# Block products of the output projection by seven in place of eight, with both weights' parts streamed

## The chip, the cores and the metric

The kernel runs on one core of one Trainium2 chip. The core has a matrix engine (PE; PEld is its loading of weights), three engines for element-wise work (DVE, ACT, POOL) and a queue, SP, from which every DMA of this kernel is issued. The metric is the device time of one execution in microseconds (us).

## The reference

```python
a = softmax(phi, over 32 slots)                    # (8 batches, 8 heads, 576 tokens, 32)
k_m, v_m = a^T k, a^T v                            # 32 slots x 64 per head
attn = softmax(q k_m^T / 8) v_m                    # (8, 8, 576, 64)
x = attn, heads side by side                       # (4608, 512)
h = x @ w_in                                       # (4608, 2048)
g = where(h > 0, h, exp(min(h, 0)) - 1)            # elu
return g @ w_out                                   # (4608, 512)
```

The weights arrive as float64; all else is float32.

## The kernel before

**Three passes.** Each large product is made of two-part numbers. A value is split into a high part (a cast to fp32r) and a low part (the value less its high part), and the product is summed over three passes: low x high, high x low, high x high. Splitting a tensor thus costs one cast on ACT and one subtraction on DVE.

**Units of work.** A batch of 576 tokens is two halves of 288. The 2048 hidden channels are 16 groups `j` of 128. One unit `it` is one (batch, half, group), and a batch is 32 units. For each unit, `hidden(it)` (L657) makes 128 channels x 288 tokens in PSUM with 6 matmuls of 288 columns. `elu_exp` (L672, L673) and `elu_max` (L684 for 256 tokens, L686 for the last 32, the "rest") form g. `elu_high` (L698) and `elu_low` (L704) split it into `gp`. `project(it)` (L712) multiplies the two 128-token blocks of `gp` with the group's 128 x 512 tile of w_out: 2 blocks x 3 passes = 6 matmuls of 512 columns. The 32-token rests of two batches are gathered and projected together after each odd batch (`rest_high`, `rest_low`, `rest_project`, 48 matmuls, then `rest_store`).

**PSUM.** `hidden` has two banks (`psh`). Its bank is free again when `elu_max` has read it. The attention has two (`psb`). The projection has four (`pso00` to `pso11`), one for each half and token block, since the halves of a batch alternate group by group.

**The product w_in with the values.** `vw` (L502) multiplies the 32 slot values of each head with w_in in four chunks `c` of 512 hidden channels (`win`, resident in SBUF); `vw_high` (L605) and `vw_low` (L611) split it. `hidden` multiplies that with the softmax `A`, so the attention's own output is never formed.

**Attention of a batch**, `attention(b, o)`: `load_phi`, `load_kv` (5 loads), `load_e` (3), `spread_max` (the slots' maxima go to DRAM as `nmd`, L276, and come back to all partitions as `nmb`, L278), `e_shift` on POOL (L289), `e_exp` on ACT (L294), `slots` on PE (L453), `scores` on PE (L502), then the softmax on DVE and ACT for three token ranges `u`.

**Order.** The list `FIRST` is a hand-written order for units 0 to 63 (batches 0 and 1, and the decoding of both weights from float64). After it, `plan` sorts every step by a place number, counted in units:

```python
    def attention(b, o):
        at(o - 4, load_phi, b)
        for c in range(NCH):
            at(o - 3 + c, load_kv, b, c)
...
        at(o + 1, spread_max, b)
...
            at(o + 5.4, slots, b, c)
```

For batch `b` with first unit `base = 32 b`, `o` is `base - 22`. PE and SP carry out their steps in exactly this order. ACT, DVE and POOL get an order from the scheduler, which may move a step ahead of an earlier one. SP issues a DMA as soon as its buffer is free and its data is there; the place numbers do not hold it back, and one that must wait holds all behind it.

Of the kernel before, what the change touches and what calls it, by code (L numbers as in the profile page):

```python
# [8 lines left out]
F32 = mybir.dt.float32  # L9
F32R = mybir.dt.float32r  # L10
# [86 lines left out]
elu_high.16 rest_copy.16 collect.14.0 elu_low.16 project.15 elu_exp.17 load_raw.15 dec_add.13
collect.14.1 elu_max.17 dec_high.13 vw.0.1.256.512 dec_top.14 rest_copy.17 collect.15.0 hidden.18
elu_high.17 dec_rest.13 collect.15.1 project.16 elu_exp.18 elu_low.17 vw_high.0.1.256.512
elu_max.18 hidden.19 dec_low.14 rest_copy.18 vw_low.0.1.256.512 elu_high.18 project.17 dec_add.14  # L100
elu_exp.19 load_raw.16 elu_low.18 dec_mag.15 load_raw.17 elu_max.19 load_raw.18 hidden.20
dec_high.14 dec_top.15 rest_copy.19 load_raw.19 elu_high.19 project.18 elu_exp.20 elu_low.19
dec_low.15 elu_max.20 vw.1.1 dec_rest.14 elu_high.20 rest_copy.20 dec_mag.16 elu_low.20 hidden.21
vw_high.1.1 dec_add.15 project.19 dec_top.16 elu_exp.21 dec_high.15 elu_max.21 load_raw.20
hidden.22 dec_mag.17 vw_low.1.1 rest_copy.21 elu_high.21 project.20 dec_low.16 elu_low.21
elu_exp.22 dec_rest.15 dec_mag.18 hidden.23 elu_max.22 dec_add.16 dec_mag.19 rest_copy.22
project.21 elu_high.22 dec_top.17 elu_exp.23 dec_mag.20 hidden.24 load_raw.21 elu_max.23
dec_low.17 elu_low.22 rest_copy.23 hidden.25 dec_top.18 elu_high.23 elu_exp.24 project.22
elu_exp.25 elu_max.24 dec_low.18 elu_max.25 rest_copy.24 hidden.26 elu_low.23 elu_high.24
rest_copy.25 elu_high.25 collect.22.0 dec_mag.21 project.23 collect.22.1 elu_exp.26 elu_low.24  # L110
elu_max.26 hidden.27 collect.23.0 elu_high.26 rest_copy.26 project.24 collect.23.1 elu_exp.27
elu_low.25 elu_low.26 elu_max.27 hidden.28 dec_add.17 elu_high.27 rest_copy.27 project.25
elu_low.27 elu_exp.28 dec_add.18 hidden.29 elu_max.28 dec_top.19 elu_high.28 rest_copy.28
project.26 elu_exp.29 elu_low.28 dec_low.19 elu_max.29 load_raw.22 hidden.30 dec_add.19
elu_high.29 rest_copy.29 project.27 elu_low.29 elu_exp.30 dec_top.20 load_raw.23 vw.1.2 elu_max.30
dec_low.20 dec_top.21 rest_copy.30 project.28 load_raw.25 elu_high.30 vw_high.1.2 dec_add.20
dec_low.21 hidden.31 vw_low.1.2 dec_high.20 project.29 elu_exp.31 elu_low.30 dec_mag.23 elu_max.31
hidden.32 dec_mag.22 dec_rest.20 rest_copy.31 elu_high.31 dec_add.21 project.30 dec_mag.25
elu_exp.32 elu_low.31 dec_top.22 dec_high.21 hidden.33 elu_max.32 project.31 dec_low.22
dec_rest.21 rest_copy.32 elu_high.32 dec_add.22 elu_exp.33 hidden.34 elu_max.33 dec_high.22  # L120
vw.0.2.0.256 elu_low.32 rest_copy.33 elu_high.33 dec_top.23 hidden.35 elu_exp.34 project.32
vw_high.0.2.0.256 elu_max.34 elu_exp.35 elu_low.33 rest_copy.34 elu_high.34 vw_low.0.2.0.256
hidden.36 dec_low.23 elu_max.35 load_raw.30 project.33 elu_low.34 elu_exp.36 rest_copy.35
dec_add.23 load_raw.24 elu_high.35 hidden.37 elu_max.36 dec_high.23 elu_low.35 rest_copy.36
elu_high.36 dec_rest.22 project.34 elu_exp.37 elu_low.36 dec_mag.30 elu_max.37 hidden.38
dec_rest.23 elu_high.37 rest_copy.37 load_raw.27 project.35 elu_low.37 elu_exp.38 dec_mag.24
dec_top.25 hidden.39 elu_max.38 dec_low.25 load_raw.28 dec_top.24 project.36 rest_copy.38
elu_high.38 elu_exp.39 elu_low.38 dec_low.24 hidden.40 elu_max.39 dec_mag.27 dec_add.25
rest_copy.39 project.37 elu_high.39 dec_add.24 elu_exp.40 dec_mag.28 load_raw.26 hidden.41
elu_max.40 load_raw.29 elu_low.39 elu_high.40 rest_copy.40 dec_top.28 project.38 elu_exp.41  # L130
elu_max.41 vw.0.2.256.512 dec_low.28 collect.38.0 rest_copy.41 project.39 elu_high.41 collect.38.1
vw_high.0.2.256.512 dec_mag.26 elu_low.40 vw_low.0.2.256.512 hidden.42 dec_mag.29 collect.39.0
project.40 elu_exp.42 collect.39.1 elu_max.42 elu_low.41 hidden.43 elu_high.42 rest_copy.42
dec_add.28 project.41 elu_exp.43 elu_low.42 dec_high.28 dec_top.30 hidden.44 elu_max.43 dec_low.30
dec_rest.28 project.42 rest_copy.43 elu_high.43 dec_top.27 elu_exp.44 hidden.45 elu_max.44
dec_low.27 vw.0.3.0.256 elu_low.43 rest_copy.44 dec_top.26 elu_high.44 hidden.46 elu_exp.45
project.43 vw_high.0.3.0.256 load_raw.31 elu_max.45 elu_exp.46 vw_low.0.3.0.256 rest_copy.45
elu_high.45 hidden.47 dec_low.26 elu_max.46 elu_low.44 rest_copy.46 elu_high.46 hidden.48
elu_low.45 elu_exp.47 elu_low.46 project.44 elu_exp.48 elu_max.47 dec_add.26 rest_copy.47
elu_max.48 hidden.49 dec_mag.31 dec_add.27 rest_copy.48 elu_high.47 project.45 load_phi.2  # L140
dec_top.29 elu_exp.49 vw.0.3.256.512 elu_max.49 dec_low.29 elu_low.47 project.46 rest_copy.49
dec_add.30 elu_high.48 vw_high.0.3.256.512 vw_low.0.3.256.512 hidden.50 dec_high.30 elu_high.49
elu_low.48 project.47 dec_rest.30 elu_exp.50 elu_low.49 elu_max.50 load_kv.2.0 hidden.51
dec_add.29 rest_copy.50 elu_high.50 dec_top.31 load_kv.2.1 dec_high.29 project.48 elu_exp.51
load_kv.2.2 elu_low.50 dec_low.31 load_kv.2.3 hidden.52 elu_max.51 dec_rest.29 elu_high.51
rest_copy.51 load_kv.2.4 project.49 elu_exp.52 elu_low.51 elu_max.52 vw.1.3 dec_add.31
# [29 lines left out]
def fused_kernel(ctx: ExitStack, tc: tile.TileContext, phiT, phi, kv0, kvt, kv, q0, q1, w_in, w_out, out):  # L176
# [22 lines left out]
    def t2k(shape, name):  # L199
        return work.tile(shape, F32, name=name, tag="t2k", bufs=7)  # L200
# [732 lines left out]
```

## Time and profile before

| | |
|---|---|
| median of 3 runs | 734.49 us (734.39 to 738.01) |
| profiled execution, its own time | 735.4 us |
| its span, first to last instruction | 733.6 us |
| PE busy | 709.2 us, 97% |
| DVE, ACT, POOL busy | 467.2, 465.0, 44.6 us |
| DMA, mean | 88 GB/s |

A line of the profile names the engine, the line of the code, what is written and read (`out<-in`), the shapes and the count. In a timeline the first column is the start, the second the time taken by the merged instructions, and a bracket at the end is idle time of the engine and what ended it. The recorded end of a matmul contains its drain, so the time that a group costs PE is read from its start to the start of the next group.

### The profile page before, as it was taken

How to read it: one execution, taken by the hardware profiler on the slowest of the kernel's cores; microseconds unless marked ns; L12 is line 12 of the kernel's file. 1: busy time of each engine (PE TensorE's matmuls, PEld its weight loads, DVE VectorE, ACT ScalarE, POOL GpSimd, SP SyncE). 2: the span in 40 equal slices, each digit the busy share in tenths (PEclk: the TensorE clock that was granted, in tenths of full speed). 3: DMA queues.
4: the chain of work that ended last, by engine and by line, in shares of the span. 5: the costliest groups of instructions: out<-in, count | busy, mean ns of one | idle time of the engine just before them, and what ended most of it. 6: DMA issues, size and time to landing. Idle time of an engine off the chain costs nothing.

```text
span 733.6 us, 13668 instructions
## 1 busy us (share of the span) xinstructions
PE 709.2 (97%) x5114; PEld 572.5 (78%) x5114; DVE 467.2 (64%) x1253; ACT 465.0 (63%) x1110; POOL 44.6 (6%) x88
## 2 busy tenths in 40 slices
PE   7688999999999999999999999999999999999997
PEld 6566888888768878877788777887787887888885
DVE  4999899886495467544954449545774447754442
ACT  4768988886456656755655557656565565665552
POOL 0001112123000100010000100000000010000000
PEclk9899999999999999999999999999999999999999
DMA  8960513431316110611015210260002600010002
GB/s 311 370 231 28 203 30 115 149 101 62 101 59 210 28 44 1 239 42 45 2 57 182 56 45 1 75 206 28 18 1 75 218 27 20 1 58 0 2 1 72
DMA packets 24978, 64.46 MB, mean 88 GB/s; under 512 B 3408, under 2 KB 7632, under 8 KB 24912
## 3 DMA queue, kind: packets, MB, share of 16 engines
q1 hardware_dynamic: 24912, 63.59, 25.7%
q8 instruction: 41, 0.67, 0.4%
q14 instruction: 25, 0.20, 0.1%
HBM read 54.13 MB, written 9.44 MB: 87 GB/s over the span
## 4 chain that ended last, share of the span: by engine, by line
PE 68%; DMA 14%; DVE 8%; ACT 5%; issue 2%; POOL 1%; SPq 1%; POOLq 0%; DVEq 0%; ACTq 0%
PE pso L712 41%; PE psh L657 21%; DMA nmd<-nm 6%; PE psb L502 4%; DMA nmb<-nmd 3%; PE psb L453 2%; DMA ph<-phiT 2%; POOL e L289 1%; DMA win<-w_in 1%; ACT gf L673 1%; DMA kvt<-kv 1%; ACT gf L672 1%; DMA e<-phi 1%; DVE gf L681 1%; DVE nm L407 1%
## 5 line engine op out<-in xcount | busy, mean ns | idle before, releaser
L712 PE MATMUL pso<-wout,gp 128*128 128x512 f32 x1728 | 449.6, 398 | 3.3 <-DVE gp L704 2.6
L712 PEld LDWEIGHTS pso<-wout,gp 128*128 128x128 f32 x1728 | 310.1, 188 | 84.2 <-ACT gf L673 13.0
L657 PEld LDWEIGHTS psh<-A,vw 128*128 128x128 f32 x1536 | 229.9, 189 | 39.5 <-issue 6.2
L657 PE MATMUL psh<-A,vw 128*128 128x288 f32 x1536 | 251.1, 299 | 8.6 <-DVE rest L686 3.8
L684 DVE SCALAR_TENSOR_TENSOR gf<-gf,psh 128x256 f32<-128x256 f32 x192 | 80.4, 419 | 130.3 <-ACT gf L673 130.0
L672 ACT ACTIVATE gf<-psh 128x288 f32<-128x288 f32 x256 | 104.7, 409 | 86.3 <-PE psh L657 84.4
L698 ACT CAST gp<-gf 128x256 fp32r<-128x256 f32 x256 | 103.4, 404 | 87.0 <-DVE gf L684 73.4
L704 DVE TENSOR_TENSOR gp<-gf,gp 128x256 fp32r<-128x256 f32 x256 | 107.6, 421 | 55.0 <-ACT gp L698 54.7
L673 ACT ACTIVATE gf<-gf 128x288 f32<-128x288 f32 x256 | 113.7, 444 | 7.8
L611 DVE TENSOR_TENSOR vw<-psb,vw 128x512 fp32r<-128x512 f32 (+2 forms) x74 | 43.3, 602 | 11.7 <-ACT vw L605 11.5
L289 POOL TENSOR_TENSOR e<-e,nmb 128x512 f32<-128x512 f32 (+1 forms) x18 | 19.7, 1122 | 377.1 <-DMA nmb<-nmd 374.8
L681 DVE SCALAR_TENSOR_TENSOR gf<-gf,psh 128x288 f32<-128x288 f32 x64 | 28.9, 452 | 18.2 <-ACT gf L673 16.9
L605 ACT CAST vw<-psb 128x512 fp32r<-128x512 f32 (+2 forms) x74 | 37.1, 522 | 2.9 <-PE psb L502 0.7
L502 PE MATMUL psb<-win,kvm 64*32 64x512 f32 (+2 forms) x592 | 36.0, 541 | 0.0
L694 POOL COPY rest<-gf 128x32 f32<-128x32 f32 x64 | 24.3, 380 | 167.6 <-DVE gf L681 167.5
L686 DVE SCALAR_TENSOR_TENSOR rest<-gf,psh 128x32 f32<-128x32 f32 x192 | 34.2, 179 | 0.1
L752 ACT CAST gp<-rest 128x256 fp32r<-128x256 f32 x32 | 13.0, 406 | 23.8 <-PE pso L712 21.8
L373 DVE SCALAR_TENSOR_TENSOR top<-mag,top 128x512 uint32<-128x512 uint32 x32 | 22.2, 692 | 1.9 <-ACT mag L364 0.3
L757 DVE TENSOR_TENSOR gp<-rest,gp 128x256 fp32r<-128x256 f32 x32 | 13.4, 418 | 15.0 <-ACT gp L752 14.9
L368 ACT ACTIVATE mag<-raw 128x512 uint32<-128x512 uint32 x30 | 20.0, 670 | 2.5 <-DVE top L373 2.5
L294 ACT ACTIVATE e<-e 128x512 f32<-128x512 f32 (+1 forms) x18 | 9.8, 559 | 16.9 <-POOL e L289 16.8
L364 ACT ACTIVATE mag<-raw 128x512 f32<-128x512 f32 x30 | 19.5, 668 | 0.4 <-DVE win L385 0.4
(96 smaller groups left out, 368.4 us busy)
## 6 DMA issues: line engine op xcount, KB each, us to landing
kvt<-kv SPq DMA_DIRECT2D x32, 512.0 KB, 7.4
out<-osb SPq DMA_DIRECT2D x16, 512.0 KB, 2.8
raw<-w_in SPq DMA_DIRECT2D x15, 512.0 KB, 6.0
raw<-w_out SPq DMA_DIRECT2D x15, 512.0 KB, 7.9
qt<-q SPq DMA_DIRECT2D x18, 384.0 KB, 4.3
ph<-phiT SPq DMA_DIRECT2D x7, 576.0 KB, 5.0
e<-phi SPq DMA_DIRECT2D x12, 256.0 KB, 6.3
qh<-q SPq DMA_DIRECT2D x4, 576.0 KB, 11.5
```

What stands on the lines that cost most here:

```text
L502: nc.tensor.matmul(outs[a][32 * j : 32 * j + 32, :], lhs[r, 32 * j : 32 * j + 32], rhs[r, j], start=True, stop=True, tile_position=(64 * a ...
L605: nc.scalar.copy(s["vw"][c][:, HI, a, n0:n1], ps)
L611: nc.vector.tensor_tensor(t[:, LO, a, n0:n1], ps, t[:, HI, a, n0:n1], ALU.subtract)
L657: nc.tensor.matmul(ps, t[:, x, g, c0 : c0 + P], s["A"][hf][:, y, g, :], start=(n == 0), stop=(n == 5),)
L672: nc.scalar.activation(gf, ps, AF.Relu, scale=-1.0)
L673: nc.scalar.activation(gf, gf, AF.Exp, scale=-1.0)
L681: nc.vector.scalar_tensor_tensor(gf, gf, -1.0, ps, ALU.add, ALU.max)
L684: nc.vector.scalar_tensor_tensor(gf[:, :n], gf[:, :n], -1.0, ps[:, :n], ALU.add, ALU.max)
L686: nc.vector.scalar_tensor_tensor(rest_of(b, j)[:, o : o + REST], gf[:, n:], -1.0, ps[:, n:], ALU.add, ALU.max)
L698: nc.scalar.copy(gp[:, HI], gs[it][:, : NT * P])
L704: eng.tensor_tensor(gp[:, LO], gf[:, : NT * P], gp[:, HI], ALU.subtract)
L712: nc.tensor.matmul(ps, gp[:, y], wout[j][:, x, :], start=(first and n == 0), stop=(last and n == 2),)
```

## The change

Batches 0 and 1 stay as they are but for where buffers lie. In batches 2 to 7:

- **Halves in turn.** All 16 groups of half 0 come before those of half 1.
- **Pairs of groups.** Two groups (256 channels) are one step. `elu_relu` runs for each, `elu_exp2` once over both (576 columns), `elu_max2` for each. `project2` is at the second unit of the pair.
- **Seven products.** The two token blocks and the two channel groups make a 2 x 2 block matrix; the tile of w_out (256 x 512) is 2 x 2 as well. `project2` forms the output from seven block products of 256 columns in place of eight: 7 x 3 passes = 21 matmuls of 256 columns, against 12 of 512. Pairs 3 and 7 of each half (`PLAIN`) and the first half of batch 2 keep 12 of 512. So 11 halves x 6 pairs = 66 pairs use seven.
- **Sums of g.** `sums` makes four 128-column sums on POOL. `direct_parts` splits three blocks (ACT and DVE, 256 and 128 columns), `sum_parts` the sums (512 columns).
- **Sums of w_out.** While units 42 to 63 and the rests of batches 0 and 1 run, `build_full`, `build_sums` (POOL, 2 of 512 and 4 of 256 columns), `build_high` (ACT, 2 of 512) and `build_low` (DVE, 2 of 512) make the four sums of each of 8 pairs, and `save_t` writes them to DRAM (1 MB each).
- **Streams.** `load_t` brings a pair's sums back before each of the 66 pairs (1 MB each) into two buffers used alternately, so it waits for the last reader of the pair before the previous one. `save_w` writes decoded w_in to DRAM, and `load_w` brings it back for each of batches 2 to 7 in 8 loads of 512 KB; `vw` is then made in two halves of 256 columns. All four `vw` chunks of a batch are now made within 16 units.
- **PSUM.** The four banks hold one half: R, C, D, S. `collect_first` and `collect_sums` take R and S after pair 6, `collect_last` adds C and D after pair 7.

Core of the diff:

```diff
-        for hf, j in turns if len(order) == 0 else [
-            (hf, j) for j in range(j0, j1) for hf in range(2)
-        ]:
+        units_of = [(hf, j) for j in range(j0, j1) for hf in range(2)]
...
+        elif b >= NB:
+            units_of = [(hf, j) for hf in range(2) for j in range(j0, j1)]
...
+    def load_t(it):
+        t = work.tile(
+            [P, 2, 4, Q], F32R, name="tt", tag=f"wb{turn_of('tt', 2)}", bufs=1
+        )
+        nc.sync.dma_start(
+            t.rearrange("p x a n -> p (x a n)").bitcast(U32), td[order[it][2] // 2]
+        )
...
+    def sums(it):
...
+        eng = nc.gpsimd
+        eng.tensor_tensor(S[:, 0], a21, a22, ALU.add)
+        eng.tensor_tensor(S[:, 2], a11, a21, ALU.subtract)
+        eng.tensor_tensor(S[:, 1], S[:, 0], a11, ALU.subtract)
+        eng.tensor_tensor(S[:, 3], a12, S[:, 1], ALU.subtract)
...
+    def project2(it):
...
+        M = {
+            1: ("R", 0, A(0), Bt(0, 0)),
+            2: ("C", 0, A(1), Bt(1, 0)),
+            3: ("C", 1, SS(3), Bt(1, 1)),
+            4: ("D", 0, A(2), TT(4)),
+            5: ("S", 0, SS(0), TT(1)),
+            6: ("R", 1, SS(1), TT(2)),
+            7: ("S", 1, SS(2), TT(3)),
+        }
+        after_rest = p == 0 and hf == 0 and b % 2 == 0
+        for n in (2, 4, 5, 7, 3, 1, 6) if after_rest else (1, 2, 4, 6, 5, 7, 3):
...
         for c in range(NVC):
-            products(b, c, base - 7.6 + 8 * c)
+            for h in range(2):
+                at(base - 13 + 4 * c + h, load_w, b, c, h)
+            products(b, c, base - 10 + 4 * c)
+    streamed = [it for it in range(1, len(order), 2) if order[it][0] >= NB and seven(it)]
+    for n, it in enumerate(streamed):
+        at(streamed[n - 2] + 1.7 if n > 1 else it - 10 + n, load_t, it)
...
+            x = it - 3.5
+            if b % 2 == 0 and hf == 0 and 1 < j < 4:
+                x = it - j - 1 + 0.665 + 0.0001 * j
+            at(x, hidden, it)
+            at(x + 0.00001, elu_relu, it)
+            if j % 2:
+                at(x + 0.00002, elu_exp2, it)
+                at(x + 0.00003, elu_max2, it - 1)
+                at(x + 0.00004, elu_max2, it)
...
+                at(x + 0.1, direct_parts, it)
+                if seven(it):
+                    at(x, sums, it)
+                    at(x + 0.2, sum_parts, it)
+                at(it + 0.6, project2, it)
```

The attention's places are unchanged (`o = base - 22`).

More of the change, by code (lines that the diff above doesn't have):

```diff
@@ L138 @@
[L138 to L143, printed above, removed]
@@ L150 @@
[L150 to L151 removed]
+save_w.0.0 save_w.0.1 scores.1.0 dec_low.7 scores.1.1.yz elu_max.4 elu_exp.2 turn.1.0 rest_copy.4
+hidden.5 elu_high.4 turn.1.1 softmax_max.1.0 vw.0.0.384.512 elu_exp.5 softmax_max.1.1
+scores.1.2.yz elu_max.2 vw_high.0.0.384.512 softmax_shift.1.0 rest_copy.2 elu_high.2
+vw_low.0.0.384.512 softmax_exp.1.0 elu_low.2 hidden.6 elu_max.5 softmax_shift.1.1 rest_copy.5
@@ new lines @@
+load_kv.2.4 project.49 elu_exp.52 elu_low.51 elu_max.52 vw.1.3 dec_add.31 rest_copy.52 elu_high.52
+phi_max.2 dec_high.31 project.50 vw_high.1.3 elu_low.52 spread_max.2 build_high.3 dec_rest.31
+phi_exp.2.0 hidden.53 vw_low.1.3 phi_exp.2.1 project.51 build_low.3 save_t.3 elu_exp.53
+slot_scale.2 build_full.4 build_sums.4 elu_max.53 hidden.54 elu_high.53 rest_copy.53 elu_low.53
+project.52 elu_exp.54 elu_max.54 hidden.55 load_e.2.0 elu_high.54 rest_copy.54 elu_low.54
+project.53 build_high.4 elu_exp.55 load_e.2.1 elu_max.55 load_q.2.1 hidden.56 elu_high.55
@@ new lines @@
+build_full.6 build_sums.6 elu_low.58 slots.2.0 elu_exp.59 project.57 load_q.2.0 elu_max.59
+elu_high.59 rest_copy.59 elu_low.59 slots.2.1 hidden.60 load_q.2.2 slots.2.2 load_w.2.0.0
+elu_exp.60 project.58 elu_max.60 elu_high.60 rest_copy.60 elu_low.60 slots.2.3 load_w.2.0.1
+build_high.6 hidden.61 slots.2.4 load_w.2.1.0 elu_exp.61 project.59 build_low.6 slots_copy.2
+save_t.6 elu_max.61 elu_high.61 rest_copy.61 build_full.7 build_sums.7 hidden.62 elu_low.61
+project.60 elu_exp.62 elu_max.62 hidden.63 elu_high.62 rest_copy.62 elu_low.62 slots_transpose.2
@@ L705, in elu_low, with seven, build_full @@
         gps[it] = gp
+        let_go("gf", it)
+    Q = CW // 2
+    NP = NJ // 2
+    PLAIN = (3, 7)
+    late = {}
+    fulls = {}
+    prods = {}
+    tts = {}
+    def seven(it):
+        b, hf, j = order[it]
+        return (b, hf) != (NB, 0) and j // 2 not in PLAIN
+    def build_full(p):
+        if "FE" not in late:
+            late["FE"] = work.tile([P, 2, 4, Q], F32, name="FE", tag="wb1", bufs=1)
+        F = late["FE"][:, 0]
+        for n in range(2):
+            w = wout[2 * p + n]
+            nc.gpsimd.tensor_tensor(
+                F[:, 2 * n : 2 * n + 2].rearrange("p a n -> p (a n)"), w[:, HI], w[:, LO], ALU.add
+            )
@@ new lines, in elu_relu, with elu_exp2, elu_max2 @@
+    def elu_relu(it):
+        if "G" not in late:
+            late["G"] = [
+                work.tile([P, 2, 2, HALF], F32, name="G", tag="osb0", bufs=2) for _ in range(2)
+            ]
+        n = it // 2 % 4
+        G = late["G"][n // 2][:, n % 2]
+        nc.scalar.activation(G[:, it % 2], gs[it], AF.Relu, scale=-1.0)
+        gs[it] = G, gs[it]
+    def elu_exp2(it):
+        G = gs[it][0].rearrange("p k n -> p (k n)")
+        nc.scalar.activation(G, G, AF.Exp, scale=-1.0)
+    def elu_max2(it):
+        b, hf, j = order[it]
+        G, ps = gs[it]
+        G = G[:, it % 2]
+        n = NT * P
+        nc.vector.scalar_tensor_tensor(G[:, :n], G[:, :n], -1.0, ps[:, :n], ALU.add, ALU.max)
+        o = (b % 2 * 2 + hf) * REST
+        nc.vector.scalar_tensor_tensor(
+            rest_of(b, j)[:, o : o + REST], G[:, n:], -1.0, ps[:, n:], ALU.add, ALU.max
+        )
```

423 lines of the change are left out of this document (298 added, 125 removed).

## The prediction

> **What bounds the kernel now.** I read the page's busy times and chain first, then PE's timeline in the steady part, then stretches of time by engine.
>
> ```profile
> span 733.6 us, 13668 instructions
> PE 709.2 (97%) x5114; PEld 572.5 (78%) x5114; DVE 467.2 (64%) x1253; ACT 465.0 (63%) x1110; POOL 44.6 (6%) x88
> PE 68%; DMA 14%; DVE 8%; ACT 5%; issue 2%; POOL 1%; SPq 1%; POOLq 0%; DVEq 0%; ACTq 0%
> q1 hardware_dynamic: 24912, 63.59, 25.7%
> ```
>
> ```profile
> 399.77 1.55 PE L712 MATMUL pso<-wout,gp 128*128 128x512 f32 x6
> 401.15 0.96 PE L657 MATMUL psh<-A,vw 128*128 128x288 f32 x6
> 401.95 1.55 PE L712 MATMUL pso<-wout,gp 128*128 128x512 f32 x6
> ```
>
> ```profile
> 145.00:160.00 15.00, 15.00 (x109) 12.29 (x108) 13.74 (x32) 12.83 (x32) 3.41 (x8) 1.00 0.34 106
> 444.00:462.00 18.00, 18.00 (x132) 14.48 (x122) 15.87 (x47) 12.41 (x30) 0.00 (x0) 1.00 0.01 1
> 600.00:690.00 90.00, 90.00 (x644) 73.03 (x644) 52.30 (x152) 54.40 (x129) 0.00 (x0) 1.00 0.06 22
> ```
>
> The columns of the last fence are PE, PEld, DVE, ACT, POOL, granted clock, DMA share, GB/s. PE has no gap: between the starts, `hidden` costs it 0.80 us and `project` 1.38. DVE and ACT have room on average (52 and 54 of 90 us), but not everywhere: while a batch's softmax runs (444 to 462), DVE is at 15.87 of 18. DMA moved 63.59 MB in 25.7% of 733.6 us, 337 GB/s while it worked. So fewer PE columns are worth their time, as long as PE still finds its operands.
>
> **1. The products (gain).** `hidden` takes 0.80/6 = 0.133 us for 288 columns, `project` 1.38/6 = 0.230 for 512: 0.43 ns a column and a fixed part of 8 ns. 256 columns come to 0.119. A pair of seven is 21 x 0.119 = 2.50 against 12 x 0.230 = 2.76, so 0.26 us less, on 66 pairs 17 us. In proportion to 512 columns (0.115) it would be 0.345 a pair, 23 us; if a narrow matmul took no less than the 288 columns do (0.133), 21 x 0.133 = 2.79 and the gain is gone. I take 17: both shapes lie on one line and 256 is next to 288. PLAIN pairs and rests are unchanged.
>
> **2. SP and the attention's chain (loss).** Before, nothing holds SP back, so a batch's loads run far ahead. The chain is in the critical path's view (start, us, what), and the first `e_exp` in the timeline:
>
> ```profile
> 227.36 8.24 DMA nmd<-nm
> 235.66 4.50 DMA nmb<-nmd
> 241.59 2.02 POOL e L289 x2
> 243.63 0.42 ACT e L294
> 255.29 2.46 PE psb L453 x80
> ```
>
> ```profile
> 169.32 0.34 SPq L276 DMA_DIRECT2D nmd<-nm  x1
> 172.48 0.33 SPq L278 DMA_DIRECT2D nmb<-nmd  x1
> 241.66 0.63 ACT L294 ACTIVATE e<-e 128x512 f32<-128x512 f32 x1 [1.99 <-POOL e L289]
> ```
>
> From the issue of `nmd` to the first `e` ready (241.66 + 0.63) it takes 14.9 us, and `slots` came 13.0 us after that. With a quiet queue `nmd` took 3.2 us (169.32 to 172.48, when SP issued `nmb`), and the same chain would be 9.9.
>
> After the change `load_t` stands in that queue. Offsets are in units from the next batch's `base`. In order, SP has `load_t` for the pair at -21 (place -25.3), `load_kv` and `load_e`, `load_t` for -19 (place -21.3), the last `load_kv`, then `spread_max` (-21). The load for -19 takes the buffer that the pair at -23 reads, so SP stands until that pair's last product with a sum, and `nmd` goes out about 1.0 us later (two issues). From there PE has only the pair's last three matmuls (0.36), five `hidden` (4.0) and two `project2` (5.0) to `slots` at -16.6: 9.4 us. So `slots` stands 1.0 + 14.9 - 9.4 = 6.5 us if `nmd` takes 8.24, and 1.5 if it takes 3.2. Ahead of `nmd` are 1 MB of sums, a `kv` of 0.25 MB and what is left of some 3.6 MB (1 of sums, 4 x 0.5, 0.6 of `e`) issued in the 8.5 us before, more like the busy case, so I take 5.5. Batch 2's attention is in `FIRST`, and batch 3's falls in the half without sums; batches 4 to 7 remain: 4 x 5.5 = 22 us, between 6 and 26. Behind `nmb` on SP wait later `load_t`s, but those pairs are two or more away.
>
> **3. The clock.** A standing PE also loses clock:
>
> ```profile
> 24.00:27.50 3.50, 3.15 (x54) 2.38 (x54) 3.40 (x7) 3.18 (x7) 0.21 (x1) 0.63 1.03 412
> ```
>
> Amid the early waits 3.5 us were granted 0.63, a loss of 1.3 us. Four long stands: 4 us, between 0 and 5. The Trainium skill (TensorE: Matmul & The Clock Gate, Part 1) says that an idle window of some 3.4 us halves the clock until a busy one has passed; by that rule four stands cost an estimated 7 us, and the sum would be 3 us higher. Half clocks in the early rows agree.
>
> **4. `load_w` behind a store.** `vw` of chunk 3 (place base + 2) needs the second half of its w_in, whose load stands at base + 0, behind `store` (base - 0.2).
>
> ```profile
> 378.98 2.58 SPq L743 DMA_DIRECT2D out<-osb  x2
> out<-osb SPq DMA_DIRECT2D x16, 512.0 KB, 2.8
> kvt<-kv SPq DMA_DIRECT2D x32, 512.0 KB, 7.4
> ```
>
> `store` waits for `collect_last`, about 1.0 us after the half's last matmul, and takes SP 1.3; the load then lands 2.8 later when alone, at about 5.1, or 5.9 behind the store's bytes. PE is at `vw` after two `hidden` and one `project2`, 4.1. So 1.0 to 1.8 us for batches 3 to 7; at 7.4 to land it would be 5.6 a batch. The queue is nearly empty there, so 1.4 x 5 = 7 us, between 0 (if PE is late anyway) and 28. The start of batch 2 is alike: its chunk 2 waits on SP behind `save_t` of the last sums and two stores, 2 us, between 0 and 4.
>
> **5. `vw` in two halves.** 512 columns cost 1.02 us from start to start, 192 (in `scores`) 0.48:
>
> ```profile
> 318.58 1.09 PE L502 MATMUL psb<-win,kvm 64*32 64x512 f32 x16
> 319.60 1.65 PE L712 MATMUL pso<-wout,gp 128*128 128x512 f32 x6
> 438.57 0.56 PE L502 MATMUL psb<-qt,kvm 64*32 64x192 f32 x16
> 439.05 1.07 PE L657 MATMUL psh<-A,vw 128*128 128x288 f32 x6
> ```
>
> Between them 256 is 0.59, twice 1.18: 0.16 more for 24 chunks, 4 us, unless the second half follows without the fixed part. I take 2, between 0 and 4.
>
> **6. The PSUM banks and DVE.** A bank of `hidden` is freed by `elu_max2`, now behind an exponential over 576 columns:
>
> ```profile
> 425.59 0.96 PE L657 MATMUL psh<-A,vw 128*128 128x288 f32 x6
> 426.59 0.41 ACT L672 ACTIVATE gf<-psh 128x288 f32<-128x288 f32 x1 [0.41 <-PE psh L657]
> 427.04 0.44 ACT L673 ACTIVATE gf<-gf 128x288 f32<-128x288 f32 x1
> 427.51 0.42 DVE L684 SCALAR_TENSOR_TENSOR gf<-gf,psh 128x256 f32<-128x256 f32 x1 [0.86 <-ACT gf L673]
> 427.85 0.18 DVE L686 SCALAR_TENSOR_TENSOR rest<-gf,psh 128x32 f32<-128x32 f32 x1
> 245.51 1.04 PE L657 MATMUL psh<-A,vw 128*128 128x288 f32 x6 [0.81 <-DVE rest L686]
> ```
>
> PE is done with `hidden` at 426.39; the bank is free 1.64 us later, at 428.03. With 288 columns more in the exponential (0.20 by the slope between the two casts below) it is 1.85, about 2.0 with the hand-over, and PE comes back for that bank after one `project2`, 2.50. Before it came back after 3.6. The last row shows such a wait already, when ACT stood behind `e`. The margin of 0.5 us is less than one cast or subtraction:
>
> ```profile
> L673 ACT ACTIVATE gf<-gf 128x288 f32<-128x288 f32 x130 | 57.7, 444 | 3.9
> L672 ACT ACTIVATE gf<-psh 128x288 f32<-128x288 f32 x131 | 53.6, 409 | 51.8 <-PE psh L657 50.7
> L698 ACT CAST gp<-gf 128x256 fp32r<-128x256 f32 x131 | 53.1, 405 | 51.7 <-DVE gf L684 49.7 <-PE pso L712 2.0
> L605 ACT CAST vw<-psb 128x512 fp32r<-128x512 f32 x32 | 18.8, 587 | 1.5
> L611 DVE TENSOR_TENSOR vw<-psb,vw 128x512 fp32r<-128x512 f32 x32 | 21.8, 682 | 8.4 <-ACT vw L605 8.3
> L289 POOL TENSOR_TENSOR e<-e,nmb 128x512 f32<-128x512 f32 x6 | 7.7, 1309 | 256.7 <-DMA nmb<-nmd 256.7
> ```
>
> Per pair of seven, ACT has 2 x 0.41 + 0.65 + 0.405 + 0.31 + 0.59 = 2.8 us (0.31 for 128 columns by the slope from 512 to 256), DVE 4 x 0.30 for the maxima + 0.42 + 0.28 + 0.68 = 2.6, in 4.1 us of PE; before they had 2.5 and 2.0 in 4.4. POOL, a quarter of 1.31 and a start, 4 x 0.45 = 1.8. All fit. In the softmax's 18 us DVE would need 15.9 + 4.4 x 0.6 = 18.5, which is over. I take 1 us for each of 5 batches, 5 us, between 0 and 19 (0.2 for each of 96 pairs).
>
> **7. The sums of w_out.** Each of 8 adds 2 x 0.587 to ACT, 2 x 0.68 to DVE and some 5.6 to POOL. POOL has room; in 145 to 160 DVE has 13.74 of 15 and three builds bring 4.1, so 2.8 too much there, some of it taken up later: 2 us, between 0 and 5. `save_w` and `save_t` are nothing while the queue has room (0.34 busy in that stretch).
>
> **8. DMA in total.** 66 MB of sums and 25 of w_in in, 12 out, and the old 64 make some 170 MB (in units of 1.05 MB for 1 MB), at 337 GB/s some 505 us of 760: not the bound. A pair's sums need 1.05/0.337 = 3.1 us and about 1.5 to land where 5.7 are at hand, two such loads a half; nothing, if no other load is ahead, and inside term 2 where one is.
>
> **Sum.** -17 + 22 + 4 + 7 + 2 + 2 + 5 + 2 = +27. The profiled execution took 735.4 (span 733.6 and 1.8 around it), 0.9 above the median, so 762 against it and about 761 as a median. With all ends at their best -23 + 6 = -17, 718; the likeliest's own range, terms 2, 4 and 6 going part of the way, is 743 to 785.
>
> **Rivals.**
> - **The waits find cover: faster.** If `nmd` finds a quiet queue and PE reaches `slots` late enough, term 2 and its clock go. Terms 4 to 7 at a third, 6 us, leave -17 + 6 = -11, 724; with 23 in place of 17, 718. It decides where the waits are under 13 us in all (17 less 0.5%). For it: DMA is idle 75% of the time; against it: the chain's 14.9 us and SP's order.
> - **The banks bound it: slower.** If half the pairs lose the margin and one cast (0.8 us on 48 pairs, 38 us) and the chain hides in that, 735.4 - 17 + 38 + 9 = 765 at most, 750 with half of it. The stretch at 15.87 of 18 speaks for it, 54.40 of 90 against.
> - **Narrow matmuls save nothing: the change does not do what it says.** At 0.133 a matmul, with the other terms, 779. The Trainium skill (TensorE: Matmul & The Clock Gate, Back-to-back issue gap) gives 81 ns at 128 columns and 131 at 512 for matmuls each with a weight load; by that an estimated 98 at 256, 0.48 us lost a pair and the sum 49 us higher. The 0.230 here differ from its 131, and the rows decide.
> - **Gain and waits cancel**: 732 to 738.
>
> **How the numbers follow.** The chain on SP 0.42, cover 0.34, the banks 0.10, narrow matmuls 0.05, cancelled 0.09. 0.5% is 3.7 us, about what a measurement of this kernel can tell from no change. Faster 0.34, within 0.09, slower 0.57. The range 716 to 783 leaves out about 0.1 of the fastest and 0.1 of the slowest.
>
> **What would show it.** Term 1: `project2` at 2.5 us from start to start of 21. Term 2: PE idle ahead of `slots` (L453), released by ACT's `e`, 4 times, with `nmd` issued right after a `load_t`. Term 4: PE idle before `vw`, released by the DMA of w_in. Term 6: PE idle before `hidden`, released by the rest's DVE line. I am wrong if `slots` never waits, or if the step at 256 columns is not near 0.119.

## The result, and the profile after

The changed kernel takes 844.7 us (median; 842.6 to 845.5) against 736.1 for the kernel before on the same chip: 1.148 times as long, 95% interval 1.145 to 1.151. That is slower, as forecast, but by 109 us where 27 were forecast. The page of the profiled execution first:

```profile
span 843.5 us, 16195 instructions
...
PE 735.7 (87%) x6092; PEld 624.7 (74%) x6092; DVE 554.3 (66%) x1349; ACT 470.2 (56%) x1066; POOL 231.2 (27%) x400
...
PEclk8899999988999998998899989899989998899999
...
q1 hardware_dynamic: 46704, 170.55, 55.8%
...
PE 35%; DVE 20%; ACT 16%; POOL 12%; DMA 11%; issue 5%; SPq 1%; DVEq 0%; POOLq 0%; ACTq 0%
```

PE was busy for 97% of the span and is now busy for 87%; it holds 35% of the chain that ended last, where it had 68. The clock row drops to 8 tenths again and again. What PE waited for, from 250 us on (batches 2 to 7):

```profile
PE psb L487 <- ACT e L328: 25.1, 4, 6.7
PE psb L536 <- DVE vw L662: 24.7, 10, 4.7
PE psh L711 <- DVE rest L849: 8.5, 21, 2.0
PE psb L536 <- DMA wt<-wd: 8.1, 5, 2.7
PE pso L912 <- DMA tt<-td: 1.7, 3, 1.1
```

The columns are total us, times and the longest. The first row is `slots` (term 2 of the prediction), the second is `scores` of the third token range standing behind `vw` of chunk 0 (no term), the third is term 6, the fourth term 4. In the kernel before, PE has one such row of over 0.4 us in these batches:

```profile
PE psh L657 <- DVE rest L686: 3.8, 5, 1.1
```

Two of the new stands and the clock around them, in the view by stretches (PE, PEld, DVE, ACT, POOL, granted clock, DMA share, GB/s):

```profile
386.00:389.00 3.00, 0.00 (x0) 0.00 (x0) 0.00 (x0) 0.61 (x1) 1.93 (x2) 0.56 0.97 406
389.00:393.00 4.00, 3.93 (x72) 3.30 (x76) 0.00 (x0) 1.06 (x3) 1.30 (x2) 0.50 0.93 371
...
412.00:416.40 4.40, 0.23 (x10) 0.00 (x0) 3.48 (x11) 2.62 (x6) 1.88 (x4) 1.00 0.89 359
416.40:420.00 3.60, 2.79 (x22) 1.77 (x23) 3.37 (x9) 0.60 (x2) 0.00 (x0) 0.59 0.33 132
420.00:424.00 4.00, 4.00 (x14) 3.52 (x14) 1.52 (x6) 1.81 (x4) 0.11 (x1) 0.51 0.00 0
```

After these stands PE works for some 4 and 6 us at half rate. In all, from the first `hidden` of batch 2 (246.2 us) on, PE worked 56.6 us at half clock, which is 28 us lost; the kernel before has no half clock once its start is over. The chain in front of `slots`, as SP issued it and as the critical path shows it:

```profile
371.46 0.33 SPq L823 DMA_DIRECT2D tt<-td  x1
...
373.45 0.54 SPq L310 DMA_DIRECT2D nmd<-nm  x1
380.83 0.32 SPq L312 DMA_DIRECT2D nmb<-nmd  x1
```

```profile
380.83 6.08 DMA nmb<-nmd
...
387.07 1.29 POOL e L323
388.38 0.64 ACT e L328
...
389.07 2.98 PE psb L487 x49
```

DVE had the maxima ready at 366.9; SP stood for the buffer of the sums until 371.5, so `nmd` left 6.6 us late.

PE's side of the second stand, and a pair's seven products ahead of it:

```profile
408.53 0.89 PE L912 MATMUL pso<-wout,GP 128*128 128x256 f32 x6
409.26 0.52 PE L912 MATMUL pso<-tt,GP 128*128 128x256 f32 x3
409.61 1.24 PE L912 MATMUL pso<-tt,gS 128*128 128x256 f32 x9
410.68 0.52 PE L912 MATMUL pso<-wout,gS 128*128 128x256 f32 x3
411.13 1.09 PE L536 MATMUL psb<-wt,kvm 64*32 64x256 f32 x32
416.73 0.58 PE L536 MATMUL psb<-qt,kvm 64*32 64x192 f32 x8 [4.50 <-DVE vw L662]
```

Nine 256-column matmuls go from 409.61 to 410.68: 0.119 us each, the forecast figure. Then `vw` of chunk 0 takes both `psb` banks, and `scores` behind it stands 4.50 us until `vw_high` and `vw_low` have emptied them.

A ledger of the 110 us between the two spans. From the first `hidden` of all to the first of batch 2 it takes 192.5 us before and 220.8 after: **28 us** are lost before batch 2, where the sums of w_out are built (2 more lie before the first `hidden`). From there to the end it is 80 more: PE's waits of over 0.4 us grew by **59**, half clock costs **28**, and the rest of its stream came out **7** shorter, where the products should have brought 17.

### The profile page after: what moved, and what is told of

Its sections match the earlier page's. It is cut to its first block, busy times and chain, and to the rows that moved or that the text cites. A ratio compares the mean times of both kernels' runs of the same rounds, so it can differ in the third digit from the quotient of the medians.

```text
span 843.5 us, 16195 instructions
## 1 busy us (share of the span) xinstructions
PE 735.7 (87%) x6092; PEld 624.7 (74%) x6092; DVE 554.3 (66%) x1349; ACT 470.2 (56%) x1066; POOL 231.2 (27%) x400
## 3 DMA queue, kind: packets, MB, share of 16 engines
q1 hardware_dynamic: 46704, 170.55, 55.8%
## 4 chain that ended last, share of the span: by engine, by line
PE 35%; DVE 20%; ACT 16%; POOL 12%; DMA 11%; issue 5%; SPq 1%; DVEq 0%; POOLq 0%; ACTq 0%
PE psh L711 13%; PE pso L992 10%; PE pso L912 8%; ACT G L840 4%; DVE G L847 4%; ACT G L835 3%; POOL GF L861 3%; ACT gS L893 3%; DMA nmb<-nmd 3%; DMA wt<-wd 3%; PE psb L487 3%; POOL GF L859 2%; POOL GF L862 2%; POOL GF L860 2%; DMA ph<-phiT 2%
## 5 line engine op out<-in xcount | busy, mean ns | idle before, releaser
L992 PE MATMUL pso<-wout,GP 128*128 128x512 f32 x504 | 139.7, 413 | 7.5 <-DVE GP L757 4.1
L847 DVE SCALAR_TENSOR_TENSOR G<-G,psh 128x256 f32<-128x256 f32 x192 | 79.8, 417 | 77.0 <-ACT G L840 76.6
L912 PE MATMUL pso<-wout,gS 128*128 128x512 f32 (+1 forms) x558 | 127.6, 365 | 0.0
L992 PEld LDWEIGHTS pso<-wout,GP 128*128 128x128 f32 x504 | 93.7, 195 | 34.4 <-DVE GP L757 6.3
L912 PEld LDWEIGHTS pso<-wout,gS 128*128 128x128 f32 x558 | 97.9, 196 | 15.7 <-issue 0.8
L835 ACT ACTIVATE G<-psh 128x288 f32<-128x288 f32 x192 | 74.3, 410 | 56.3 <-PE psh L711 54.6
L912 PE MATMUL pso<-tt,gS 128*128 128x256 f32 x594 | 81.8, 282 | 0.0
L912 PEld LDWEIGHTS pso<-tt,gS 128*128 128x128 f32 x594 | 75.5, 190 | 0.0
L887 DVE TENSOR_TENSOR GP<-G,GP 128x128 fp32r<-128x128 f32 (+1 forms) x132 | 58.6, 476 | 18.9 <-ACT GP L885 18.6
L840 ACT ACTIVATE G<-G 128x576 f32<-128x576 f32 x96 | 65.8, 685 | 2.9
L912 PEld LDWEIGHTS pso<-wout,GP 128*128 128x128 f32 x396 | 52.9, 188 | 0.0
L487 PE MATMUL psb<-kvt,e 128*32 128x128 f32 (+1 forms) x480 | 23.3, 362 | 25.1 <-ACT e L328 25.1
L757 DVE TENSOR_TENSOR GP<-GF,GP 128x256 fp32r<-128x256 f32 x64 | 37.1, 582 | 9.4 <-ACT GP L751 9.3
```

The costliest lines, as they stand in the source:

```text
L487: nc.tensor.matmul(ps[32 * j : 32 * j + 32, a], s["e"][c // 2][:r, c % 2, x : x + M], kv_rows(b, c, i, 2 * j + a), start=(c == 0 and a == ...
L835: nc.scalar.activation(G[:, it % 2], gs[it], AF.Relu, scale=-1.0)
L840: nc.scalar.activation(G, G, AF.Exp, scale=-1.0)
L847: nc.vector.scalar_tensor_tensor(G[:, :n], G[:, :n], -1.0, ps[:, :n], ALU.add, ALU.max)
L887: nc.vector.tensor_tensor(f(LO), src, f(HI), ALU.subtract)
L912: nc.tensor.matmul(banks[bank_name][:, c0:c1], lhs(y), rhs(x), start=bank_name not in seen_banks, stop=stop and n == 2, skip_group_check=True,
```

## The experiments

Each was timed beside the kernel before, on several chips (its medians are 733.9 to 737.0 us), so 3 us between two runs on different chips mean nothing. Line numbers shift by a few between them. Theory A: separate waits, each with a half clock. Rival B: a crowded engine or queue, which turns each removed wait into another.

**The wait of `slots`.** Four kernels start its chain earlier.

`e1_chain`:

```
-        at(o - 4, load_phi, b)
+        at(o - 9, load_phi, b)
...
-        at(o + 0.1, phi_max, b)
+        at(o - 6, phi_max, b)
...
-        at(o + 1, spread_max, b)
+        at(o - 5, spread_max, b)
```

> The changed kernel, with SP's loads and copies of the maxima (load_phi, phi_max, spread_max) five or six places earlier in the order, so that they no longer stand behind the stream of block sums. Theory A (the time is lost in separate waits, each followed by a stretch at half clock): the four waits of slots for e, 25.1 us in the changed kernel, go, and with them the half clock after each, about 4 us at half rate, 2 us apiece; 844.7 - 25 - 8 = 812 us (805 to 820). Rival B (a crowded engine or full PSUM banks set the pace in batches 2 to 7, and whatever wait is removed comes back in front of the next bound): less than half of it, 832 us or more, with longer waits for rest or for vw.

Measured 845.7 us: nothing gained, though `slots` no longer waits at all. PE's waits, and its timeline at one of the new ones, with ACT's just before:

```profile
PE psh L711 <- DVE rest L849: 25.2, 20, 4.2
...
PE pso L912 <- DMA tt<-td: 9.5, 4, 2.9
```

```profile
377.78 0.52 PE L912 MATMUL pso<-wout,gS 128*128 128x256 f32 x3
381.88 2.38 PE L711 MATMUL psh<-A,vw 128*128 128x288 f32 x11 [3.59 <-DVE rest L849]
```

```profile
379.54 0.63 ACT L328 ACTIVATE e<-e 128x512 f32<-128x512 f32 x1 [2.60 <-POOL e L323]
380.08 0.39 ACT L835 ACTIVATE G<-psh 128x288 f32<-128x288 f32 x1
```

The exponential of `e` now stands earlier in ACT's order, waits there for POOL, and the relu of the hidden blocks waits behind it. The page names DVE's rest as PE's releaser, but that is only the end of the row: ACT is late, and what ACT waits for is a DMA two steps back. POOL waited for `e` to land.

`e5_early_e` moves that load too:

```
-            at(o - 3 + u, load_e, b, u)
+            at(o - 8.9 + 0.1 * u, load_e, b, u)
```

> e1_chain, with the three loads of phi for e (load_e) moved ahead too, right behind load_phi. In e1_chain the wait of slots was gone, and ACT stood 2.6 us behind e_exp, which waited for POOL's shift, which waited for e to land 9.2 us after its issue; the relu of the hidden blocks stood behind it and TensorE waited 3 to 4 us for a bank. Theory A (one late transfer, seen through in-order queues): with e there early nothing is left to wait for, and the 25 us and some 8 us of half clock are gained at last: 815 us (806 to 822). Rival B (the DMA queue is full in this stretch, and any load that is moved ahead delays another): the waits pass to tt and kvt, 835 us or more.

Measured 847.0 us. POOL, ACT and PE at one of its waits:

```profile
373.78 1.29 POOL L323 TENSOR_TENSOR e<-e,nmb 128x512 f32<-128x512 f32 x1 [3.46 <-DMA nmb<-nmd]
```

```profile
375.10 0.63 ACT L328 ACTIVATE e<-e 128x512 f32<-128x512 f32 x1 [4.20 <-POOL e L323]
```

```profile
381.05 3.22 PE L711 MATMUL psh<-A,vw 128*128 128x288 f32 x12 [6.55 <-DVE rest L849]
```

Now it is `nmb` that is late, and POOL stands for it between two additions of `sums`. Both DMAs of the chain now stand ten places ahead of `slots`, yet POOL's and ACT's orders, which the scheduler fixes in advance, had followed them forward.

`e9_chain2` starts four places earlier still (`load_phi` at `o - 13`, `phi_max` at `o - 10`, `spread_max` at `o - 9`):

> e5_early_e, with load_phi, phi_max, spread_max four places earlier still. In e5_early_e the copy of the maxima was issued at 361.2, the broadcast at 367.8, and POOL waited for it until 373.8 us, between two of its additions for the products; ACT waited 4.2 us for POOL with relu and exponentials of the next pair behind it, and TensorE 6.55 us. Theory A (one late broadcast behind in-order queues): four places are some 9 us, more than these waits, and nothing stands behind it now: 815 us (805 to 822). Rival B (the DMA queue and the engines are full, and a wait comes back as another): 835 us or more.

Measured 835.1 us: B, at its lower edge. `slots` no longer waits, `nmb` is in time and rest waits 12.1 us (37.8 in `e5_early_e`); now SP is late:

```profile
346.86 0.83 SPq L310 DMA_DIRECT2D nmd<-nm  x1
352.43 0.32 SPq L312 DMA_DIRECT2D nmb<-nmd  x1
...
354.43 12.43 SPq L823 DMA_DIRECT2D tt<-td  x3
```

```profile
PE pso L912 <- DMA tt<-td: 17.9, 4, 6.3
```

The issue of `nmb` waits 5.6 us for `nmd` to land, with the streams of sums behind it. `e13_split` therefore issues the two apart (`spread_rest` is the second transfer of `spread_max`, `nmb`):

```
+        if b > 2:
+            at(o - 4.6, spread_rest, b)
```

> e9_chain2, with the two transfers of spread_max apart: the copy of the maxima to DRAM at the same place, the broadcast back four places later. In e9_chain2 SP stood 5.6 us behind the broadcast (346.9 to 352.4 us), which waits for the copy to land, with the streams of block sums behind it, and TensorE waited 17.9 us for tt. Theory A (whatever stands on an in-order queue behind this round trip pays for it): with no queue standing, the waits of slots, rest and tt are gone together: 835 - 18 - 5 (clock) = 812 us (805 to 820). Rival B: the wait comes back once more in another place, 828 us or more.

Measured 828.1 us, at the edge of B. `slots` and `tt` wait 2 us together; rest waits 13.8 us in batches 2 to 7 where it had 8.5, and `vw` waits 13.5 for `wt` where it had 8.1. Half clock costs 30 us from batch 2 on (28 in the changed kernel), so A's gain in the clock did not come. So term 2's wait was 25 us long and it took four moves of one small round trip to get 17 us of it: a wait that SP, POOL or ACT has to make in order is paid by whatever is queued behind it.

**`scores` behind `vw`.** `e2_vw0`:

```
-            products(b, c, base - 10 + 4 * c)
+            products(b, c, base - 10 + 4 * c if c else base - 8.3)
```

> The changed kernel, with vw of chunk 0 of a batch at place base - 8.3 in place of base - 10, behind the third scores in place of right ahead of it. Theory A: the five waits of scores for vw's low parts, 22.8 us in the longest five, go, and about 2 us of half clock with each; 844.7 - 23 - 10 = 812 us (805 to 820). Rival B: the banks are short wherever vw stands, so vw waits for turn, or hidden for vw, in its place: 832 us or more.

Measured 820.0 us: 24.6 gained by one move in PE's order. The wait of `scores` (24.7) is gone and half clock falls from 34 to 17 us lost (from 60 us on); rest waits 22.4 us in place of 8.5, since DVE has no room while the softmax runs (third number, 22.73 of 28):

```profile
397.00:425.00 28.00, 24.65 (x246) 21.16 (x247) 22.73 (x63) 16.94 (x40) 6.66 (x12) 1.00 0.67 251
```

A holds for the wait and the clock, B for the 14 us that came back.

**The builds.** `e3_noadds` makes POOL's additions for pair 0 alone:

```
     def build_full(p):
+        if p:
+            return
...
     def build_sums(p):
+        if p:
+            return
```

> The changed kernel, with POOL's additions for the block sums of w_out made for the first pair alone; the other seven pairs' sums are split and stored from the same numbers, so the output is not the reference's. DVE's and ACT's part of the builds and the stores stay. Theory C (POOL's two-input additions stretch DVE's two-input operations while they run): DVE's L757 and L811 between 145 and 260 us go back to their durations of before, and most of the 30 us by which batch 2 starts late goes: 820 us (814 to 828). Rival D (the builds' own work on DVE and ACT fills an already full DVE): 838 us or more.

Measured 835.9 us: between C and D. Batch 2 starts 213.2 us after the first `hidden` (220.8 after the change). DVE beside POOL in the changed kernel, DVE first:

```profile
153.61 0.69 DVE L431 TENSOR_TENSOR wout<-top,wout 128x512 fp32r<-128x512 f32 x1
...
157.84 1.49 DVE L757 TENSOR_TENSOR GP<-GF,GP 128x256 fp32r<-128x256 f32 x1
159.25 1.50 DVE L406 TENSOR_SCALAR top<-raw 128x512 uint32<-128x512 uint32 x1
...
161.81 0.44 DVE L735 SCALAR_TENSOR_TENSOR GF<-GF,psh 128x288 f32<-128x288 f32 x1
...
163.20 0.41 DVE L757 TENSOR_TENSOR GP<-GF,GP 128x256 fp32r<-128x256 f32 x1
```

```profile
157.34 3.13 POOL L789 TENSOR_TENSOR FE<-wout 128x512 f32<-128x512 f32 x2
```

While POOL adds (157.34 to 160.5), L757 takes 1.49 us, where it takes 0.41 when it starts between two additions (163.20), and L406 1.50 for 0.43. The operation that reads PSUM (161.81) keeps its 0.44 beside POOL's next additions. In the whole trace L757 takes 0.96 us in the median of the 19 that overlap an addition and 0.42 in that of the 45 others. The Trainium skill (Trainium Architecture — The Big Picture, "What this means for kernel authors") says that DVE and GpSimd contend for one shared SBUF port pair, as an exclusive lock. These rows agree. Without the additions another wait shows, ACT's for the only buffer of the split sums:

```profile
ACT tt L808 <- DMA td<-tt: 11.4, 3, 8.6
```

The changed kernel has it too, with 4.9 us.

`e7_nostores` leaves that out too: no stores for pairs 1 to 7, every stream reads pair 0's sums.

```
     def save_t(p):
+        if p:
+            tts.pop(("new", p))
+            return
...
```

> e3_noadds, with the stores of the block sums of pairs 1 to 7 left out too, and every stream reading the stored sums of pair 0, so the output is not the reference's. In e3_noadds ACT waited 11.4 us (8.6 in one) at build_high for the store of the sums before to leave their only buffer, and the elu steps queued behind it. Theory E (that wait is the larger half of the late start of batch 2): 824 us (817 to 830), batch 2 within 8 us of where it started before the change. Rival D (the splits on ACT and DVE cost the rest): 833 us or more.

Measured 828.1 us, in E's range, but batch 2 starts at 204.2, which is 11.7 late where E had 8 at most. Additions and stores together are 16.6 of the 28 us, the splits and the rest of the stage 11.7. `e12_plain` below, which builds no sums at all, starts batch 2 at 195.4, so most of the 28 us belongs to the builds. `e4_dve` puts the additions on DVE (`nc.gpsimd` to `nc.vector` in both functions):

> The changed kernel, with the additions for the block sums of w_out on DVE in place of POOL. Theory C: DVE gets some 15 us of work (8 x (2 x 0.42 + 4 x 0.25) by its own rows) and loses the stretch; where it has room, from 180 us on, that is hidden, in the first three builds it is not: 832 us (825 to 840). Rival D: DVE is the bound of this stage, so its 15 us come on top: 855 us (848 to 865).

Measured 842.0 us: neither theory's size. DVE's own additions cost about what POOL's had cost beside it. The 15 us expected were too few: in this trace an addition takes 0.68 us at 512 columns and 0.41 at 256, which makes 24 us for the eight builds. `e8_six` drops the sums of pairs 3 and 7, which nothing reads, and takes the places of builds 3 to 7 in the written order for pairs 0, 1, 2, 4, 5:

```
+    for n, f in enumerate((build_full, build_sums, build_high, build_low, save_t)):
+        at(66 + 0.5 * n, f, 6)
```

> The changed kernel, with the sums of pairs 3 and 7, which no product reads, not built, and the six others built some ten units later, where the rows of the kernel before show DVE at half load (8.9 of 20 us) against 18 of 20 earlier. Theories C and E: the contention and the wait for the buffer cost less with a quarter less work in a quieter stretch: batch 2 starts some 18 us earlier, 826 us (820 to 833). Rival: the same waits come back there, against the softmax and the rests: 838 us or more.

Measured 832.3 us, at the edge of C and E: 12.4 gained. Batch 2 starts at 209.1, 11.7 earlier where 18 were expected.

**Edits together.** `e6_three` is `e5_early_e`, `e2_vw0` and the last loads of w_in ahead of the store:

```
-                at(base - 13 + 4 * c + h, load_w, b, c, h)
+                at(base - 13 + 4 * c + h if c < 3 else base - 4.6 + 2 * h, load_w, b, c, h)
```

> The changed kernel, with the edits of e5_early_e and e2_vw0 and the last two loads of w_in of a batch (chunk 3) ahead of the store they stood behind. Theory A (separate waits): e2_vw0 gave 25 us, e5_early_e would give 30, and the 8 us of vw's waits for wt go with some 2 us of clock: 844.7 - 25 - 30 - 10 = 780 us (770 to 792). Rival B: 805 us or more, as the DMA queue and DVE take up what is removed.

Measured 813.5 us: B. Against `e2_vw0` only the wait for `wt` is gained; the 22.8 us of `slots` are gone too, and rest waits 46.2 where it had 22.4. `e10_all` is `e9_chain2`, `e2_vw0`, `e8_six` and these loads:

> The edits of e9_chain2, e2_vw0 and e8_six and the early loads of chunk 3 together. Theory A: the gains add: 844.7 - 30 (chain) - 25 (vw) - 12 (builds) - 8 (wt) = 770 us (760 to 782). Rival B: DVE, which was full for 25 us around each softmax in e2_vw0, holds it: 790 us or more.

Measured 795.0 us: B. PE still waits 19.4 for `tt` (SP behind the round trip) and 23.1 for rest. `e11_all_dve` adds the builds on DVE:

> e10_all, with the additions of the six builds on DVE in place of POOL. DVE gets 6 x (2 x 0.69 + 4 x 0.42) = 18 us, in a stretch where it had 10 of 20 us free, and POOL's additions, beside which its own two-input operations took 1.3 to 1.8 us in place of 0.42 to 0.68, are gone. Theory C: 3 to 10 us below e10_all. Rival D: 5 us or more above it.

Measured 789.9 us: C, by 5 us, in a stretch where DVE has room. `e15_all_split` issues `nmd` and `nmb` apart, as `e13_split` does:

> e11_all_dve (seven products, early vw of chunk 0 moved, early loads of chunk 3, six builds on DVE), with the early maxima's two transfers apart. Theory A: the 18.5 us of waits for tt go and some 5 us of half clock: 766 us (758 to 774). Rival B: 783 us or more.

Measured 780.2 us, between A and B. `e16_late_builds` has three builds (4, 5, 6) behind the start of batch 2, at units 66, 69.5 and 73, and the first loads at `it - 4`:

> e15_all_split, with three of the six builds behind the start of batch 2 (from units 66, 69.5 and 73), and the first two streams of sums later by six units. In e11_all_dve batch 2 started 15.5 us late against the kernel before, while DVE held builds, rests and softmax. Theory C (a crowded DVE there, with room behind it): 5 to 10 us below e15_all_split. Rival: the softmax of batch 3 is crowded as well, within 3 us of it or above it.

Measured 776.4 us, 3.8 below `e15_all_split` and so just short of C's gain; it is the best with seven products (with `e18_late_pin` below): 1.056 times the kernel before (1.053 to 1.059). Its PE waits:

```profile
PE psh L715 <- DVE rest L853: 30.4, 37, 3.7
PE pso L916 <- DMA tt<-td: 6.4, 5, 2.3
```

From batch 2 on it loses 4 us to half clock where the changed kernel lost 28. What remains is many short waits for DVE: from batch 2 on PE waits 30 us more than in the kernel before, against the 17 that the products were to bring.

**Without the seven products.** `e12_plain` has eight products everywhere, without the builds, `collect_first` and `collect_sums`, and with the edits of `e2_vw0` and of the last loads:

```
-    PLAIN = (3, 7)
+    PLAIN = tuple(range(8))
...
```

> The changed kernel with eight block products everywhere: no block sums, no streams of them, no sums of the hidden units, one full pair of output banks; halves in turn, w_in streamed from DRAM, and the edits of e2_vw0 and of chunk 3 stay. Theory F (what the seven products need costs all that is lost, halves in turn and the streamed w_in little): no saving of 17, waits of slots gone as no stream holds SP, no late start of batch 2: 745 us (736 to 757). Rival G (halves in turn and streamed w_in lose by themselves): 765 us or more.

Measured 762.1 us, near G: 14 us faster than the best with seven products and 25 slower than the kernel before. PE's largest wait in it, and ACT's:

```profile
PE psh L711 <- DVE rest L849: 20.0, 9, 4.2
```

```profile
ACT e L328 <- POOL e L323: 25.2, 11, 4.4
```

The kernel before has ACT's stand as well:

```profile
ACT e L294 <- POOL e L289: 16.8, 9, 3.3
```

In batches 2 to 7 of `e12_plain` ACT stands 3.5 to 4.4 us for POOL's `e` once in each of five batches, and PE waits 1.9 to 4.2 us right behind, 15.2 of the 20.0 us. In the kernel before ACT stands 2.0 to 3.3 us at the same place, and PE waits 0.5 to 1.1.

`e14_plain_split` gives it the early maxima of `e13_split`:

> e12_plain (eight products), with the early maxima and the two transfers apart as in e13_split. In e12_plain POOL waited for the broadcast until 431.8 us, ACT 4.2 us for POOL, TensorE 4.2 us, and so once in each batch, with 8 us of half clock in all. Theory A: 762 - 15 - 6 = 741 us (735 to 748), so that halves in turn and the streamed w_in cost next to nothing. Rival G (they do cost): 753 us or more.

Measured 778.2 us, slower still, on G's side. ACT and PE:

```profile
330.50 0.63 ACT L335 ACTIVATE e<-e 128x512 f32<-128x512 f32 x1 [8.20 <-POOL e L330]
```

```profile
333.64 3.22 PE L718 MATMUL psh<-A,vw 128*128 128x288 f32 x12 [8.19 <-DVE rest L856]
```

SP issued `nmd` at 316.7 and `nmb` at 323.6, and POOL had it at 329.2: a round trip of 12.5 us. POOL has nothing else to do here. As I read these rows, and no run shows it by itself, nothing held the shift and the exponential of `e` to their own place, and they went into ACT's order right after the transfers, ahead of a round trip that takes longer than the order allows for. `e17_plain_pin` ties the shift to a hidden block:

```
+    def pin(b, it):
+        x = st[b]["nmb"][:, 0, 0:1]
+        nc.vector.scalar_tensor_tensor(x, gs[it][:, 0:1], 0.0, x, ALU.mult, ALU.add)
...
+            at(o + 1.500005, pin, b, 2 * NJ * b - 17)
```

> e14_plain_split (eight products), with the shift of e tied to TensorE: one DVE step adds zero times a column of the hidden block of unit base - 17 to the broadcast maxima, so POOL's shift and ACT's exponential can't be put ahead of that place. In e14_plain_split the exponential of e had been put into ACT's order some eight units ahead of its own place, as soon as the order's planner held the early broadcast to be there, and ACT stood 8.2 us. Theory A (ACT's order follows the maxima wherever they are moved, and stands for the part of their 12 us round trip that the planner leaves out): with the place tied down the wait goes: 778 - 28 - 9 = 741 us (736 to 748). Rival G: halves in turn and the streamed w_in cost by themselves, 753 us or more.

Measured 772.4 us, G's number, but the tie did not do what it was meant to, so this decides nothing. At most 6 us are gained (1.047 to 1.059 times the kernel before, after 1.055 to 1.061). The tie stands at `o + 1.5`, behind the first of the three shifts (`o + 1.1`), which stayed free. In the trace two of the long waits remain (6.8 and 7.2 us), again with ACT standing for that shift (7.59 us at the first). `e18_late_pin` has the same tie on `e16_late_builds`:

> e16_late_builds (seven products with all the edits so far), with the same tie. There the waits that come from ACT or POOL standing for the maxima are 1.5 to 2.3 us a batch, and as much for tt. Theory A: 776 - 10 = 766 us (760 to 771). Rival B (DVE's crowd sets the pace, whatever ACT does): 773 us or more.

Measured 776.3 us, nothing gained: B. There most of the waits are for DVE's rest (31.4 us, 40 times).

No version beats the kernel before.

## Why the prediction was right or wrong

The side was right, and so were three terms in place and size (2, 4, 8); term 6 came near its number by luck. The sum was 82 us short. Three terms make some 75 of it (3, 5 and 7), and term 1 another 9. Neither of the two signs of being wrong came, `slots` waited and the step was 0.119, yet the time lies 62 us above the range: the signs watched the terms that I had listed, and not the steps that the change moves.

- **Term 1, the products**: the step at 256 columns is 0.119 as forecast. Of the 17 us, the trace gives 8: the steps of all product matmuls of batches 2 to 7, waits over 0.4 us left out, add up to 307.4 us before and 299.2 in `e16_late_builds`, where the clock hardly disturbs. There the step from a pair's last product to the next `hidden` is 0.32 us on average (33 times), where a step inside a pair is 0.12; with such short waits ahead of the attention's products this keeps some 6 us of the rest.
- **Term 2, SP and the chain**: 22 forecast, 25.1 measured, 4 times, right behind a `load_t`. The mechanism was right. Not foreseen was that this wait has no cheap cure: `e1_chain` and `e5_early_e` removed it and gained nothing.
- **Term 3, the clock**: 4 forecast, 28 measured in batches 2 to 7. The step that failed is "four long stands" at 1 us each. There were nine of over 4 us in the batches, and twelve stretches of half clock, 2.4 us lost in each. In the 20 traces of this study, after the first 60 us, half clock followed all 101 stands of 4 us or more, 24 of the 30 between 3 and 4 us and 33 of the 55 between 2 and 3 us, but none of the 117 between 0.8 and 1.2 us. The Trainium skill (TensorE: Matmul & The Clock Gate, Part 1) says that an idle window of some 3.4 us brings half clock. The long stands agree, and the traces add that shorter ones count too.
- **Term 4, `load_w`**: 7 forecast, 8.1 measured.
- **Term 5, `vw` in two halves**: costed as time per matmul, and that is small (24.8 us against 22.4 for all of them). What I missed is the place: the change moves `vw` of chunk 0 from base - 7.6 to base - 10, and the third `scores` is at base - 9.8. Both use both banks of `psb`, and I gave the move no cost. `e2_vw0` shows 24.7 us of wait and, with the clock, 24.6 us of time.
- **Term 6, banks**: 5 forecast; rest waits went from 3.8 to 8.5. That the number fits is luck: PE stood elsewhere. As the other waits went, rest waits grew to 22.4 us (`e2_vw0`) and 30.4 (`e16_late_builds`), above the term's upper end of 19. The term also left out that POOL's `sums` slow DVE in most pairs: the 128-column subtraction of `direct_parts` (L887) takes 0.55 us beside them (52 of 66) and 0.28 otherwise. What that costs PE was not tested.
- **Term 7, the builds**: 2 forecast, 28 lost before batch 2, most of it to the builds. "POOL has room" was the step that failed: POOL had room, but DVE was slowed beside it, and the single buffer held ACT for a store: leaving out the additions starts batch 2 7.6 us earlier (`e3_noadds`), the stores another 9.0 (`e7_nostores`). I added their durations as if the engines did not touch.
- **Term 8**: 170 MB forecast, 170.55 moved; not the bound in total. But landing times grew where loads bunch, and in `e1_chain` 1 MB of sums took 12.1 us to land in the 30 us around `slots`.

That a removed wait came back as another is shown in full by `e1_chain` and `e5_early_e`, and in part by `e9_chain2`, `e2_vw0` and `e15_all_split`. Open is the cause of the 25 us that `e12_plain` loses without seven products. From batch 2 on its PE waits 16 us more than in the kernel before and loses 8 us to half clock, which is nearly all. Most of these waits follow ACT's stand for the maxima. Such stands are there in the kernel before, some 1 us shorter, and cost PE little, which suggests that the pairs leave less room to cover them; that was not tested. In the runs that moved or tied the maxima the stand was not removed cleanly, so it was not shown that halves in turn and the streamed w_in cost nothing by themselves.

## What to carry to other kernels

Before costing what a change adds, list for every step that it moves which banks and buffers the step takes and which step stands next in that engine's order: a move without a new instruction cost 25 us here. A transfer that an in-order queue has to wait for is paid by whatever stands behind it, so removing one wait shows little until no queue stands for the slow step, and an order fixed in advance follows a transfer that is moved ahead. Count a TensorE stand of 4 us or more with another 2 us for the half clock behind it, and one of 2 to 4 us with about two thirds of that (57 of 85 were followed by it here).

## What the runs showed of the hardware

- DVE subtractions with both inputs in SBUF took up to 3.6 times as long beside POOL's two-input additions (L757, 1.51 for 0.42 us); the operation with an input from PSUM kept its time (L735, 0.43 to 0.46 us in the 14 that overlap an addition).
- The half clock began by the end of the stand in 84 of the 101 stands of 4 us or more and at most 0.9 us behind it in the other 17. It lasts one or more steps of 3.41 us: two in 69 of the 85 stands of 4.5 us or more.
- A round trip of 1 KB through DRAM and back to 128 partitions took 12.5 us in a busy queue (`e14_plain_split`: 6.9 to the issue of the broadcast, 5.6 to its arrival).
